# Recurrence and gated MLP on one core: from the ninth chunk on, score matmuls and output matmuls of two chunks stand next to each other

## The chip, the cores and the metric

One core of one Trainium2 chip. The metric is the device time of one execution in microseconds (us); the times given are of the whole program, the trace is of one profiled execution.

## The reference

A linear recurrence over 768 steps for 4 batches and 8 heads of 48, and behind it a gated MLP over the 3072 rows that come out.

```
for t in range(S):                       # S = 768, per batch and head, state is 48 x 48
    cur = einsum(u * k[t], v[t])
    y[t] = einsum(r[t], state + cur)
    state = w[t][:, None] * state + einsum(k[t], v[t])
x = y as (3072, 384)
out = (silu(x @ w_gate) * (x @ w_val)) @ w_out      # 384 -> 1536 -> 384
```

## The kernel before

**The recurrence** is cut into 24 chunks of 128 steps. Chunk n is chunk n // 4 of batch n % 4, so four chunks in a row belong to four batches and don't need each other; chunk n needs the state that chunk n - 4 left. For a chunk the names in the code are:

- `ws`, `kr`, `nat`, `vt`: the loads of decay, keys and receptances, the same in natural order, values.
- `scan`, `seed`, `kq`, `scan2`, `re`: running products of the decay and what is scaled by them, on DVE; `ru`, `ruk`, `a0`: the bonus on the diagonal, on DVE; `zero`: a small memset on POOL.
- `diag` (ACT): writes the diagonal into two tiles `at`, one for each half of the heads. `sc` (PE): the scores, 32 matmuls with 48 rows and 64 columns of the array, into two PSUM banks (j = 0 and 1). `pred` (DVE): copies the lower triangle of one score bank into `at`, in three instructions (L518 once, L524 twice); with that the bank is free.
- `kb` (PE, four transposes), `kn` (ACT, its copy), `dl` (PE, 32 small matmuls): the state's increment. `sps` (DVE) scales the state, `spb` (ACT) copies it into the zero-padded tile `sp`, `st` (DVE) adds the increment, with which the bank of `dl` is free.
- `vz` (ACT): a zero-padded copy of part of the values. `y` (PE): the output of the chunk, 56 matmuls of 32 columns. `xh` (ACT) and `xl` (DVE): the output split in a high and a low part, with which the bank of `y` is free.

**The MLP** runs over seven groups of 4, 2, 4, 4, 4, 4 and 2 chunks (`GROUPS`), each in twelve steps f. `gv` (PE): nine matmuls of 128 by 128 with 512 columns (256 for a group of 2), twice, for gate and value. `silu` and `hh` (ACT), `sg` and `hl` (DVE) make the product and split it. `po` (PE): three matmuls with 384 columns for each chunk of the group, added up over f in one PSUM bank for each chunk. `ob` and `out` bring out the group's result. `raw`, `top`, `low`, `shift`, `sign`, `plus`, `upper`, `lower` turn the weights' 64-bit bits into two parts while the first group runs; the bits lie in two buffers `raw` of 9216 bytes a partition.

**PSUM** has eight banks: two `pa` (for `kb`, `y`, `dl`), two `gv` (for the gate and value products and, from chunk 6 on, for `sc`), four `po`.

**The order** of all this is one table, `ORDER`, of 1495 words such as `gv:2:5:0` (group, step, gate or value) or `sc:13` (chunk). Every engine gets its instructions in the order of this table; nothing is moved later. `spin:6` stands for six matmuls whose result nobody reads.

Of the kernel before, what the change touches and what calls it, by code (L numbers as in the profile page):

```python
# [52 lines left out]
top:1 spin:7 wm:0:0 wl:0:0 kn:2 diag:2:1 zero:2 prod:3 scan:3 wm:0:2 wl:0:2 wm:0:1 wl:0:1 y:1 xh:1
sc:2 dl:2 xm:1 diag:2:0 raw:2 vt:3 ws:4 kr:4 kq:3 shift:1 seed:3 sign:1 plus:1 pred:2:0 pred:2:1
st:2 spin:2 kb:3 xl:1 low:2 whole:3 gv:0:0:0:a gv:0:0:1:a upper:1 scan2:3 kn:3 vz:2 wm:1:1 zero:3
y:2 silu:0:0:a diag:3:1 re:3 sc:3 sg:0:0:a scan:4 xh:2 diag:3:0 pred:3:1 pred:3:0 wm:1:2 wm:1:0
hh:0:0:a vz:3 top:2 hl:0:0:a prod:4 wl:1:2 whole:4 y:3 xh:3 seed:4 raw:3 po:0:0:c0 xm:2 xm:3
po:0:0:c1 wl:1:1 xl:2 xl:3 dl:3 wl:1:0 gv:0:0:0:b top:3 shift:2 sign:2 gv:0:0:1:b kq:4 plus:2
silu:0:0:b upper:2 scan2:4 sg:0:0:b hh:0:0:b low:3 gv:0:1:0:a kb:4 gv:0:1:1:a lower:2 hl:0:0:b
silu:0:1:a shift:3 sg:0:1:a po:0:0:c3 gv:0:1:0:b gv:0:1:1:b hh:0:1:a vt:4 vt:5 sign:3 ws2:0 kn:4  # L60
vz:4 check2:0 hl:0:1:a raw:4 plus:3 silu:0:1:b po:0:1:a prod:5 raw:5 upper:3 sg:0:1:b hh:0:1:b re:4
top:4 lower:3 po:0:0:c2 shift:4 gv:0:2:0 st:3 low:4 gv:0:2:1 hl:0:1:b silu:0:2 diag:4:0 sc:4 sign:4
sps:4 sg:0:2 diag:4:1 hh:0:2 plus:4 pred:4:0 pred:4:1 raw:6 gv:0:3:1 gv:0:3:0 upper:4 spb:4 lower:4
hl:0:2 dl:4 y:4 ws:5 top:5 silu:0:3 xh:4 low:5 shift:5 sign:5 sg:0:3 po:0:1:b plus:5 zero:4 hh:0:3
hl:0:3 scan:5 upper:5 po:0:2 lower:5 gv:0:4:0 top:6 silu:0:4 low:6 shift:6 xm:4 gv:0:4:1 gv:0:5:1
sign:6 sg:0:4 ws2:4 plus:6 whole:5 hh:0:4 xl:4 upper:6 raw:7 kq:5 raw:8 hl:0:4 top:7 lower:6 po:0:3
gv:0:5:0 shift:7 kb:5 silu:0:5 sg:0:5 sign:7 st:4 seed:5 low:7 vz:5 plus:7 gv:0:6:1 gv:0:6:0 scan2:5
zero:5 po:0:4 hh:0:5 kn:5 diag:5:1 top:8 upper:7 hl:0:5 lower:7 low:8 silu:0:6 shift:8 sg:0:6 sign:8
raw:9 po:0:5 hh:0:6 diag:5:0 gv:0:7:1 gv:0:7:0 plus:8 hl:0:6 re:5 upper:8 silu:0:7 lower:8 top:9
sg:0:7 sps:5 spb:5 po:0:6 gv:0:8:1 sc:5 gv:0:8:0 low:9 hh:0:7 raw:10 nat:6 shift:9 sign:9 plus:9  # L70
upper:9 kr:7 pred:5:1 pred:5:0 ws:6 vt:6 dl:5 y:5 raw:11 hl:0:7 kr:6 top:10 silu:0:8 lower:9
check2:4 sg:0:8 low:10 shift:10 sign:10 hh:0:8 plus:10 po:0:7 scan:6 upper:10 xh:5 top:11 hl:0:8
lower:10 gv:0:9:1 ws:7 gv:0:9:0 silu:0:9 po:0:8 shift:11 low:11 ub vt:7 sign:11 sg:0:9 gv:0:10:0
plus:11 hh:0:9 gv:0:10:1 xm:5 whole:6 upper:11 hl:0:9 kq:6 lower:11 po:0:9 xl:5 silu:0:10 ru:6
sg:0:10 ruk:6 gv:0:11:0 seed:6 scan2:6 hh:0:10 vz:7 zero:6 hl:0:10 silu:0:11 re:6 a0:6 kb:6
gv:0:11:1 kn:6 diag:6:0 sg:0:11 scan:7 hh:0:11 hl:0:11 po:0:10 dl:6 sc:6 sps:6 pred:6:0 diag:6:1
spb:6 nat:7 po:0:11:c2 po:0:11:c1 vz:6 gv:1:0:0 pred:6:1 ob:0:2 ru:7 st:6 seed:7 ws:8 silu:1:0
gv:1:0:1 kq:7 sg:1:0 hh:1:0 whole:7 ruk:7 hl:1:0 scan2:7 a0:7 po:0:11:c3 gv:1:1:0 gv:1:1:1
po:0:11:c0 out:0:2 y:6 zero:7 silu:1:1 ob:0:1 sg:1:1 diag:7:1 re:7 sc:7 po:1:0:c0 po:1:0:c1 nat:8
scan:8 hh:1:1 pred:7:1 sps:7 whole:8 diag:7:0 kr:8 hl:1:1 ru:8 pred:7:0 ruk:8 st:5 gv:1:2:0 po:1:1  # L80
seed:8 gv:1:2:1 spb:7 xh:6 silu:1:2 xl:6 sg:1:2 gv:1:3:0 a0:8 ws2:3 hh:1:2 hl:1:2 gv:1:3:1 silu:1:3
sg:1:3 hh:1:3 po:1:2 gv:1:4:0 gv:1:4:1 kq:8 hl:1:3 scan2:8 silu:1:4 gv:1:5:0 sg:1:4 hh:1:4 re:8
hl:1:4 kb:7 kn:7 ob:0:0 y:7 silu:1:5 diag:8:1 dl:7 st:7 diag:8:0 sc:8 pred:8:1 pred:8:0 po:1:3 sps:8
spb:8 gv:1:5:1 sg:1:5 zero:8 gv:1:6:0 po:1:4 hh:1:5 xh:7 ws:9 kb:8 scan:9 gv:1:6:1 nat:9 vt:9 vt:8
kr:9 seed:9 hl:1:5 whole:9 check2:3 ru:9 po:1:5 xl:7 vz:8 silu:1:6 gv:1:7:0 ruk:9 a0:9 sg:1:6
gv:1:7:1 hh:1:6 vz:9 kn:8 kq:9 hl:1:6 silu:1:7 scan2:9 y:8 dl:8 sg:1:7 ws:10 ws:11 diag:9:1 hh:1:7
nat:10 diag:9:0 zero:9 re:9 vt:10 hl:1:7 st:8 sc:9 sps:9 spb:9 pred:9:1 pred:9:0 kb:9 po:1:6 out:0:0
out:0:1 gv:1:8:0 gv:1:8:1 silu:1:8 kn:9 sg:1:8 hh:1:8 ru:10 hl:1:8 gv:1:9:1 gv:1:9:0 po:1:7 scan:10
ob:0:3 silu:1:9 xh:8 ruk:10 sg:1:9 seed:10 xl:8 y:9 dl:9 st:9 xh:9 xl:9 gv:1:10:0 gv:1:10:1 hh:1:9
hl:1:9 a0:10 kr:10 po:1:8 silu:1:10 po:1:9 whole:10 out:0:3 kq:10 sg:1:10 hh:1:10 scan2:10 gv:1:11:0  # L90
zero:10 hl:1:10 re:10 po:1:10 gv:1:11:1 silu:1:11 vt:11 nat:11 scan:11 ru:11 sg:1:11 hh:1:11 vz:10
diag:10:0 whole:11 gv:2:0:0 gv:2:0:1 hl:1:11 po:1:11:c0 po:1:11:c1 silu:2:0 diag:10:1 sg:2:0 ws2:6
ruk:11 seed:11 hh:2:0 gv:2:1:1 gv:2:1:0 hl:2:0 a0:11 kr:11 diag:11:0 silu:2:1 ob:1:1 sg:2:1 hh:2:1
check2:6 ob:1:0 po:2:0:c2 po:2:0:c0 nat:12 gv:2:2:0 ru:12 ruk:12 kq:11 hl:2:1 ws2:5 silu:2:2
gv:2:2:1 po:2:0:c3 sg:2:2 po:2:0:c1 sc:10 kb:10 sps:10 spb:10 kn:10 hh:2:2 scan2:11 pred:10:0 re:11
hl:2:2 po:2:1 pred:10:1 a0:12 check2:5 vz:11 gv:2:3:1 gv:2:3:0 ws2:2 ws:12 y:10 silu:2:3 xh:10
diag:11:1 sg:2:3 sps:11 spb:11 dl:10 st:10 hh:2:3 sc:11 kb:11 zero:11 pred:11:1 kn:11 pred:11:0
hl:2:3 po:2:2 gv:2:4:0 gv:2:4:1 silu:2:4 sg:2:4 xl:10 diag:12:0 gv:2:5:1 hh:2:4 dl:11 y:11 check2:2
# [6 lines left out]
pred:13:0 hl:2:7 xl:12 vt:15 vz:13 gv:2:8:0 gv:2:8:1 diag:14:1 silu:2:8 whole:14 sg:2:8 kq:14
scan2:14 dl:13 y:13 st:13 xh:13 xl:13 nat:15 zero:14 hh:2:8 re:14 gv:2:9:1 hl:2:8 diag:14:0 check:14
ws:15 ru:15 scan:15 gv:2:9:0 silu:2:9 po:2:7 sg:2:9 kr:15 kb:14 kn:14 sc:14 hh:2:9 vt:14 sps:14
pred:14:1 seed:15 spb:14 po:2:8 pred:14:0 hl:2:9 ruk:15 kq:15 whole:15 scan2:15 gv:2:10:0 out:1:1
re:15 a0:15 gv:2:10:1 silu:2:10 check:15 diag:15:1 vz:14 vz:15 po:2:9 sg:2:10 nat:16 hh:2:10 dl:14
st:14 y:14 hl:2:10 sps:15 zero:15 sc:15 pred:15:1 kb:15 diag:15:0 kn:15 pred:15:0 po:2:10 gv:2:11:0  # L110
spb:15 silu:2:11 gv:2:11:1 sg:2:11 ru:16 hh:2:11 xh:14 hl:2:11 ws:16 kr:16 gv:3:0:0 gv:3:0:1
po:2:11:c2 po:2:11:c1 scan:16 xl:14 silu:3:0 po:2:11:c3 sg:3:0 ob:2:1 hh:3:0 dl:15 y:15 po:2:11:c0
st:15 ob:2:2 xh:15 xl:15 gv:3:1:0 whole:16 ruk:16 hl:3:0 seed:16 gv:3:1:1 po:3:0:c0 silu:3:1 sg:3:1
kq:16 out:2:1 scan2:16 out:2:2 ws:17 vt:16 hh:3:1 po:3:0:c3 gv:3:2:1 gv:3:2:0 ob:2:0 ob:2:3 hl:3:1
silu:3:2 a0:16 nat:17 re:16 zero:16 ru:17 sg:3:2 diag:16:1 diag:16:0 po:3:0:c1 po:3:0:c2 hh:3:2
gv:3:3:0 hl:3:2 po:3:1 gv:3:3:1 silu:3:3 po:3:2 ruk:17 sg:3:3 check:16 hh:3:3 hl:3:3 out:2:3 sps:16
# [722 lines left out]
```

## Time and profile before

| | us |
|---|---|
| median of 3 runs | 569.04 (568.2 to 569.2) |
| the profiled execution's own time | 566.06 |
| its span in the trace | 564.4 |
| PE busy | 555.5 (98%) |
| PEld (weight loads, beside the matmuls) busy | 485.3 (86%) |
| DVE busy | 335.0 (59%) |
| ACT busy | 280.4 (50%) |

The span is the time from the first to the last instruction of one execution. A matmul's duration in the trace reaches to the modelled end of its pipeline, so neighbours overlap and a busy share of PE hides short pauses; the distance from one start to the next shows them.

### The profile page before, as it was taken

Reading aid. Unit: us, or ns where it says so; the run is one execution under the profiler, and the core shown is the slowest. Engines: PE = TensorE matmul, PEld = TensorE weight load, DVE = VectorE, ACT = ScalarE, POOL = GpSimd, SP = SyncE. Lnnn points to the kernel's source line nnn. Section 1 sums busy time; section 2 is a strip of 40 time slices with the busy share of each in tenths; the row PEclk is TensorE's granted clock in tenths of the full one; section 3 lists DMA queues with packets and bytes.
Section 4 is the critical chain, followed back from the end, with each engine's and each line's share of the span. In section 5 each row is a group of like instructions: output and inputs, shape, how many; then the busy total and the mean of one; then the engine's idle time right before and its main releaser. Section 6 shows DMA issues by size and latency. Waiting matters only on the chain.

```text
span 564.4 us, 12505 instructions
## 1 busy us (share of the span) xinstructions
PE 555.5 (98%) x5167; PEld 485.3 (86%) x5167; DVE 335.0 (59%) x602; ACT 280.4 (50%) x647; POOL 4.5 (1%) x35
## 2 busy tenths in 40 slices
...
GB/s 285 274 162 164 202 168 220 118 59 81 125 151 95 83 58 130 93 62 79 61 42 78 66 72 51 65 132 1 120 16 65 91 27 32 0 1 1 29 30 33
DMA packets 41598, 51.09 MB, mean 91 GB/s; under 512 B 12416, under 2 KB 30208, under 8 KB 41536
## 3 DMA queue, kind: packets, MB, share of 16 engines
...
q8 instruction: 42, 0.69, 0.5%
...
## 4 chain that ended last, share of the span: by engine, by line
PE 75%; DMA 1%; DVE 1%; SPq 0%; issue 0%; DVEq 0%
PE gv L625 43%; PE po L664 22%; PE y L576 5%; PE sc L500 2%; PE kb L472 1%; PE dl L544 1%; DMA nat<-in_nat_dram 1%; SPq L371 0%; DVE nat L438 0%; DVE ob L680 0%; DVE at L524 0%; DVE nat L441 0%; DVE at L518 0%; DVE x L603 0%; DVE st L553 0%
## 5 line engine op out<-in xcount | busy, mean ns | idle before, releaser
L625 PE MATMUL gv<-x,w_h 128*128 128x512 f32 (+1 forms) x984 | 282.6, 362 | 0.4 <-DVE sg L638 0.4
L625 PEld LDWEIGHTS gv<-x,w_h 128*128 128x128 f32 x984 | 176.5, 188 | 29.9 <-issue 1.5
L625 PE MATMUL gv<-x,w_l 128*128 128x512 f32 (+1 forms) x492 | 177.0, 360 | 0.0
L638 DVE TENSOR_TENSOR sg<-sg,gv 128x512 f32<-128x512 f32 (+1 forms) x82 | 49.9, 608 | 133.7 <-PE gv L625 83.9
L625 PEld LDWEIGHTS gv<-x,w_l 128*128 128x128 f32 x492 | 92.5, 188 | 12.3
L635 ACT ACTIVATE sg<-gv 128x512 f32<-128x512 f32 (+1 forms) x82 | 43.9, 535 | 118.1 <-PE gv L625 100.3
L664 PE MATMUL po<-w_h,hh 128*128 128x384 f32 x280 | 96.4, 344 | 0.0
L664 PE MATMUL po<-w_h,hl 128*128 128x384 f32 x280 | 94.4, 337 | 0.0
L664 PE MATMUL po<-w_l,hh 128*128 128x384 f32 x280 | 94.2, 336 | 0.0
L643 ACT ACTIVATE hh<-sg 128x512 fp32r<-128x512 f32 (+1 forms) x82 | 46.4, 566 | 94.4 <-DVE sg L638 82.5
L648 DVE TENSOR_TENSOR hl<-sg,hh 128x512 fp32r<-128x512 f32 (+1 forms) x82 | 49.8, 608 | 24.0 <-ACT hh L643 23.5
L664 PEld LDWEIGHTS po<-w_h,hh 128*128 128x128 f32 x280 | 52.5, 188 | 2.8 <-issue 0.4
L664 PEld LDWEIGHTS po<-w_h,hl 128*128 128x128 f32 x280 | 52.6, 188 | 1.8
L664 PEld LDWEIGHTS po<-w_l,hh 128*128 128x128 f32 x280 | 52.5, 188 | 0.0
L388 DVE TENSOR_TENSOR_SCAN qt<-ws,d 112x516 f32<-112x516 f32 x24 | 29.5, 1228 | 10.5 <-DMA ws<-in_wt_dram 10.2
L410 DVE TENSOR_TENSOR_SCAN et<-ws,d 112x516 f32<-112x516 f32 x24 | 29.5, 1229 | 1.9 <-ACT pend L393 1.3
L457 ACT ACTIVATE at<-ident,a 128x128 f32<-128x128 f32 x72 | 24.7, 392 | 10.6 <-PE y L576 8.8
L518 DVE COPY_PREDICATED at<-masks,sc 128x256 f32<-128x256 uint32 x36 | 16.1, 447 | 18.6 <-PE sc L500 16.7
L576 PE MATMUL y<-at,vz 128*32 128x128 f32 x384 | 25.3, 273 | 0.0
L454 ACT ACTIVATE at<-ident,a 128x128 f32<-128x128 f32 x72 | 24.6, 390 | 0.0
L524 DVE COPY_PREDICATED at<-masks,sc 64x128 f32<-64x128 uint32 x72 | 21.2, 295 | 0.5
L576 PEld LDWEIGHTS y<-at,vz 128*32 128x32 f32 x384 | 20.9, 110 | 0.0
...
## 6 DMA issues: line engine op xcount, KB each, us to landing
...
```

What stands on the lines that cost most here:

```text
L388: keep(nc.vector.tensor_tensor_scan(_flat(qts[n])[:, ::-1], wss[n][:, 1:][:, ::-1], _flat(d1)[:, ::-1], 0.0, ALU.mult, ALU.add))
L410: keep(nc.vector.tensor_tensor_scan(_flat(ets[n]), wss[n][:, :L], _flat(d1), 0.0, ALU.mult, ALU.add))
L454: keep(nc.scalar.activation(a[:, p, :], ident, AF.Copy, scale=d))
L457: keep(nc.scalar.activation(o, i[:, ::-1], AF.Copy, scale=d))
L524: keep(nc.vector.copy_predicated(a[o, p, :e], m.unsqueeze(1).to_broadcast([e, TWO, e]), s[o, p, :e],))
L576: pin(nc.tensor.matmul(ys[n][32 * q : 32 * q + 32, b // 4, :], lhs, rhs, start=start[q] == i, stop=stop[q] == i,))
L625: pin(nc.tensor.matmul(ps, a[:, f, j, q * P : (q + 1) * P], x[:, q, lo * P : hi * P], start=m == 0, stop=m == 3 * NK - 1,))
L635: keep(nc.scalar.activation(sgs[g, f, h], ps, AF.Silu))
L638: keep(nc.vector.tensor_tensor(sgs[g, f, h], sgs[g, f, h], gvs.pop((g, f, 1, h)), ALU.mult))
L643: keep(nc.scalar.activation(hhs[g, f, h], t, AF.Copy))
L648: keep(nc.vector.tensor_tensor(hls[g, f, h], t, hhs[g, f, h].bitcast(F32), ALU.subtract))
L664: pin(nc.tensor.matmul(pos[g, j], a[:, ts], x[:, f, 2, :], start=f == 0 and i == 0, stop=f == NF - 1 and i == 2,))
```

## The change

It concerns chunks from 8 on (`PAIRED`). Chunks 8 and 9, 10 and 11, up to 22 and 23 go through PE two at a time: the scores of both stand next to each other in `ORDER`, later the outputs of both and, where a state still has to be carried on, the increments of both. For that, the two chunks need buffers side by side: the odd chunk's scores go to the two `pa` banks, all increments from chunk 8 on go to the `gv` banks, and a second set of SBUF tiles (two `kr`, two `vt`, two `vz`, one `at`, one `kn`, one `sp`) is laid into the two `raw` buffers once the weights are converted. Three POOL memsets clear `vz` and `sp` there. No instruction of the chunks or of the MLP is added or removed; two more `spin` matmuls stand in the first stage (42 for 40). The table `ORDER` is another one from its 13th word on.

```diff
+PAIRED = 8
 ORDER = """
-ws:0 kr:0 scan:0 whole:0 spin:8 uh seed:0 prod:0 kq:0 spin:1 kb:0 scan2:0 kn:0 diag:0:0 kr:1 ws:1
...
-gv:2:7:1 scan2:13 spb:12 zero:13 hl:2:6 silu:2:7 dl:12 y:12 diag:13:1 re:13 st:12 sg:2:7 hh:2:7
-sc:13 ruk:14 kb:13 sps:13 spb:13 a0:14 kn:13 check:13 po:2:6 pred:13:1 scan:14 kr:14 seed:14 xh:12
...
+sps:12 sg:2:6 scan2:14 a0:14 sc:13 sc:12 pred:13:0 pred:13:1 po:2:5 check:14 kb:13 diag:12:0 spb:12
+pred:12:1 kr:15 vt:14 kn:13 hh:2:6 pred:12:0 y:13 y:12 dl:13 dl:12 nat:15 ws:15 vt:15 xh:13 hl:2:6
...
+    lates = {}
+    def late(name):
+        if not lates:
+            for i, parts in enumerate((
+                (("kr0", 2 * NPR * C), ("kr1", 2 * NPR * C), ("vz0", NPR * 48)),
+                (("at", NPR * C), ("kn", NPR * PR), ("sp", 2 * NPR * D), ("vt0", H * D), ("vt1", H * D), ("vz1", NPR * 48)),
+            )):
+                t = wst.tile([P, 3, DM, 2], I32, tag="raw", name=f"late_{i}")
+                t, lo = t.rearrange("p i c t -> p (i c t)").bitcast(F32), 0
+                for k, w in parts:
+                    lates[k], lo = t[:, lo : lo + w], lo + w
+            for k in ("vz0", "vz1", "sp"):
+                keep(nc.gpsimd.memset(lates[k], 0.0))
+        return lates[name]
+    def apart(n):
+        return n >= PAIRED and n % 4 > 1
...
     def kr(n):
+        if apart(n):
+            krs[n] = late(f"kr{n % 2}")[:PR].rearrange("d (i p c) -> d i p c", i=2, p=NPR)
...
-            own = (psA, "pa", 2) if n < SCORED else (psM, "gv", 2)
+            own = (psA, "pa", 2) if n < SCORED or n >= PAIRED and n % 2 else (psM, "gv", 2)
...
-        dls[n] = psA.tile([P, NPR, D], F32, tag="pa", name=f"dl_{n}")
+        own = (psA, "pa", 2) if n < PAIRED else (psM, "gv", 2)
+        dls[n] = own[0].tile([P, NPR, D], F32, tag=own[1], name=f"dl_{n}", bufs=own[2])
```

**PE at chunks 12 and 13.** Before, the last output matmuls of chunk 12 stand ahead of the first score matmuls of chunk 13; chunk 12's own scores were a stretch of their own that ended 54 rows earlier.

```order
L576 MATMUL y_12_3017<-at_12_0_2724,vt_12_2835 32x128
L576 MATMUL y_12_3017<-at_12_0_2724,vz0_95 32x128
L576 MATMUL y_12_3017<-at_12_1_2912,vt_12_2835 32x128
L576 MATMUL y_12_3017<-at_12_1_2912,vz0_95 32x128 x4
L500 MATMUL sc_13_0_3056<-kr_13_2929 64x128
L500 MATMUL sc_13_1_3057<-kr_13_2929 64x128
L500 MATMUL sc_13_0_3056<-kr_13_2929 64x64
```

With the change the scores of chunk 13 are followed by those of chunk 12, and these by the MLP's `po`:

```order
L534 MATMUL sc_13_0_2950<-kr_13_2646 64x128
L534 MATMUL sc_13_1_2951<-kr_13_2646 64x128
L534 MATMUL sc_12_0_2968<-kr_12_2541 64x128
L534 MATMUL sc_12_1_2969<-kr_12_2541 64x128
L534 MATMUL sc_12_0_2968<-kr_12_2541 64x64
...
L534 MATMUL sc_12_1_2969<-kr_12_2541 64x128
L704 MATMUL po_2_0_2529<-w_h_109,hh_2_5_2909 128x384
```

In one stretch there are now 64 score matmuls; the outputs of both chunks and then their increments follow in another, behind `po:2:5` and the transposes `kb:13`:

```order
L616 MATMUL y_13_3033<-late_1_1900,vt_13_2679 32x128
L616 MATMUL y_13_3033<-late_1_1900,vz1_97 32x128 x4
L616 MATMUL y_12_3062<-kr_12_2541,sp_93 32x128 x12
...
L616 MATMUL y_12_3062<-at_12_1_2939,vz0_95 32x128 x4
L584 MATMUL dl_13_3091<-vt_13_2679,late_1_1900 32x48 x3
...
L584 MATMUL dl_12_3108<-vt_12_2642,kn_12_2907 16x48
L503 MATMUL kb_14_3143<-ident_81,late_0_1899 128x112 x4
L665 MATMUL gv_2_7_0_3148<-x0_2_1659,w_h_109 128x512
```

**DVE at chunks 8 and 9.** Before, chunk 9's score banks are read by two `pred` (rows L518 and L524), between the state's update and the product of the MLP's step 8:

```order
L553 TENSOR_TENSOR st_0_111<-dl_8_2063,st_0_111 112x192
L530 TENSOR_TENSOR st_1_112<-st_1_112,pend_108 112x192
L518 COPY_PREDICATED at_9_1_2085<-masks_86,sc_9_1_2111 128x4x64
L524 COPY_PREDICATED at_9_1_2085<-masks_86,sc_9_1_2111 64x2x64 x2
L518 COPY_PREDICATED at_9_0_2096<-masks_86,sc_9_0_2110 128x4x64
L524 COPY_PREDICATED at_9_0_2096<-masks_86,sc_9_0_2110 64x2x64 x2
L638 TENSOR_TENSOR sg_1_8_2170<-sg_1_8_2170,gv_1_8_1_2160 128x256
```

With the change four `pred` stand in a row; chunk 8's banks, which the MLP's next products need, are read by the first and the third of them:

```order
L688 TENSOR_TENSOR hl_1_8_2096<-sg_1_8_2072,hh_1_8_2083 128x256
L552 COPY_PREDICATED at_8_1_1909<-masks_86,sc_8_1_2099 128x4x64
L558 COPY_PREDICATED at_8_1_1909<-masks_86,sc_8_1_2099 64x2x64 x2
L552 COPY_PREDICATED at_9_0_2040<-masks_86,sc_9_0_2116 128x4x64
L558 COPY_PREDICATED at_9_0_2040<-masks_86,sc_9_0_2116 64x2x64 x2
L552 COPY_PREDICATED at_8_0_1923<-masks_86,sc_8_0_2098 128x4x64
L558 COPY_PREDICATED at_8_0_1923<-masks_86,sc_8_0_2098 64x2x64 x2
L552 COPY_PREDICATED late_1_1900<-masks_86,sc_9_1_2117 128x4x64
L558 COPY_PREDICATED late_1_1900<-masks_86,sc_9_1_2117 64x2x64 x2
L466 TENSOR_TENSOR nat_10_2055<-nat_10_2055,u_bc_106 128x384
L678 TENSOR_TENSOR sg_1_9_2165<-sg_1_9_2165,gv_1_9_1_2167 128x256
```

Two `pred` more stand between a score stretch and the DVE's next step for the MLP.

## Rows read from the trace of the kernel before

**Rows 1.** The page: busy us (share of the span) and instructions.

```profile
PE 555.5 (98%) x5167; PEld 485.3 (86%) x5167; DVE 335.0 (59%) x602; ACT 280.4 (50%) x647; POOL 4.5 (1%) x35
```

**Rows 2.** Waits of PE: us in total, times, longest.

```profile
PE gv L625 <- DVE sg L638: 0.4, 1, 0.4
PE kb L472 <- issue: 0.3, 1, 0.3
PE kb L472 <- ACT st L551: 0.2, 1, 0.2
```

**Rows 3.** Timeline of PE (start, duration), increments and output of a chunk between products.

```profile
302.44 0.40 PE L625 MATMUL gv<-x,w_l 128*128 128x512 f32 x1
302.68 0.39 PE L625 MATMUL gv<-x,w_h 128*128 128x512 f32 x1
303.00 0.54 PE L544 MATMUL dl<-vt,kn 128*32 128x48 f32 x32
303.36 0.83 PE L576 MATMUL y<-kr,sp 112*32 112x128 f32 x24
...
305.00 0.50 PE L625 MATMUL gv<-x,w_h 128*128 128x512 f32 x1
305.33 0.39 PE L625 MATMUL gv<-x,w_l 128*128 128x512 f32 x1
```

**Rows 4.** Timeline of PE, scores of a chunk by themselves.

```profile
331.80 0.34 PE L664 MATMUL po<-w_h,hl 128*128 128x384 f32 x1
331.98 0.34 PE L664 MATMUL po<-w_l,hh 128*128 128x384 f32 x1
332.25 0.90 PE L500 MATMUL sc<-kr 48*64 48x128 f32 x32
333.08 0.60 PE L472 MATMUL kb<-ident,kr 112*128 112x112 f32 x4
333.45 0.42 PE L664 MATMUL po<-w_h,hh 128*128 128x384 f32 x1
```

**Rows 5.** Timeline of PE, output, increments and scores in one stretch.

```profile
396.89 0.86 PE L576 MATMUL y<-kr,sp 112*32 112x128 f32 x24
397.57 0.28 PE L576 MATMUL y<-at,vt 128*32 128x128 f32 x1
...
398.44 0.52 PE L544 MATMUL dl<-vt,kn 128*32 128x48 f32 x32
398.90 0.90 PE L500 MATMUL sc<-kr 48*64 48x128 f32 x32
399.73 0.44 PE L664 MATMUL po<-w_h,hh 128*128 128x384 f32 x1
400.01 0.33 PE L664 MATMUL po<-w_h,hl 128*128 128x384 f32 x1
```

**Rows 6.** Timeline of PE, first output matmuls of a chunk and the scores behind them.

```profile
256.74 0.83 PE L576 MATMUL y<-kr,sp 112*32 112x128 f32 x24
...
258.38 0.90 PE L500 MATMUL sc<-kr 48*64 48x128 f32 x32
```

**Rows 7.** Timeline of PE, increments ahead of the MLP's products.

```profile
165.08 0.52 PE L544 MATMUL dl<-vt,kn 128*32 128x48 f32 x32
165.53 0.39 PE L625 MATMUL gv<-x,w_h 128*128 128x256 f32 x1
```

**Rows 8.** Timeline of DVE, the two `pred` of chunk 9.

```profile
156.75 0.45 DVE L518 COPY_PREDICATED at<-masks,sc 128x256 f32<-128x256 uint32 x1 [0.21 <-PE sc L500]
...
157.73 0.45 DVE L518 COPY_PREDICATED at<-masks,sc 128x256 f32<-128x256 uint32 x1
158.08 0.60 DVE L524 COPY_PREDICATED at<-masks,sc 64x128 f32<-64x128 uint32 x2
```

**Rows 9.** Timeline of PE, the products `gv:1:8:0` behind those scores.

```profile
158.13 0.28 PE L625 MATMUL gv<-x,w_h 128*128 128x256 f32 x1
```

**Rows 10.** Timeline of PE, spins in the first stage.

```profile
12.30 1.46 PE L701 MATMUL idle<-masks 128*128 128x512 bf16 x6
```

More of the change, by code (lines that the diff above doesn't have):

```diff
@@ L53 @@
[L53 to L98, printed above, removed]
@@ L105 @@
[L105 to L116, printed above, removed]
@@ L158 @@
[L158 to L162 removed]
+ws:0 kr:0 scan:0 whole:0 spin:8 uh seed:0 prod:0 kq:0 spin:1 kb:0 scan2:0 zero:0 kn:0 diag:0:0 kr:1
@@ new lines @@
+diag:2:0 raw:2 vt:3 ws:4 kr:4 kq:3 shift:1 seed:3 sign:1 plus:1 pred:2:0 pred:2:1 st:2 spin:3 kb:3
+xl:1 low:2 whole:3 gv:0:0:0:a gv:0:0:1:a upper:1 scan2:3 zero:3 kn:3 vz:2 wm:1:1 y:2 silu:0:0:a
+diag:3:1 re:3 sc:3 sg:0:0:a scan:4 xh:2 diag:3:0 pred:3:1 pred:3:0 wm:1:2 wm:1:0 hh:0:0:a vz:3 top:2
+hl:0:0:a prod:4 wl:1:2 whole:4 y:3 xh:3 seed:4 raw:3 po:0:0:c0 xm:2 xm:3 po:0:0:c1 wl:1:1 xl:2 xl:3
+dl:3 wl:1:0 gv:0:0:0:b top:3 shift:2 sign:2 gv:0:0:1:b kq:4 plus:2 silu:0:0:b upper:2 scan2:4 zero:4
@@ new lines @@
+sg:0:0:b hh:0:0:b low:3 gv:0:1:0:a kb:4 gv:0:1:1:a lower:2 hl:0:0:b silu:0:1:a shift:3 sg:0:1:a
+po:0:0:c3 gv:0:1:0:b gv:0:1:1:b hh:0:1:a vt:4 vt:5 sign:3 ws2:0 kn:4 vz:4 check2:0 hl:0:1:a raw:4
+plus:3 sps:4 silu:0:1:b po:0:0:c2 ws:5 po:0:1:a sg:0:1:b top:4 gv:0:2:1 upper:3 re:4 hh:0:1:b
+gv:0:2:0 scan:5 lower:3 hl:0:1:b shift:4 sign:4 st:3 diag:4:1 silu:0:2 low:4 sg:0:2 sc:4 hh:0:2
+plus:4 spb:4 raw:5 hl:0:2 pred:4:1 upper:4 top:5 whole:5 po:0:1:b gv:0:3:1 lower:4 shift:5 sps:5
+gv:0:3:0 raw:6 low:5 silu:0:3 dl:4 po:0:2 diag:4:0 sign:5 sg:0:3 hh:0:3 low:6 vz:5 seed:5 plus:5
@@ new lines @@
+sg:0:7 sign:9 po:0:6 hh:0:7 plus:9 kr:7 vt:7 hl:0:7 kq:6 top:10 gv:0:8:0 gv:0:8:1 upper:9 ru:6
+silu:0:8 lower:9 sg:0:8 shift:10 po:0:7 kb:6 raw:11 low:10 hh:0:8 xh:5 kn:6 ws2:3 gv:0:9:0 gv:0:9:1
+hl:0:8 sign:10 plus:10 ruk:6 silu:0:9 upper:10 dl:6 po:0:8 top:11 sg:0:9 vz:6 lower:10 shift:11
+low:11 gv:0:10:1 gv:0:10:0 sign:11 hh:0:9 plus:11 hl:0:9 seed:6 check2:3 upper:11 a0:6 lower:11
+whole:6 po:0:9 xm:5 silu:0:10 sg:0:10 scan2:6 hh:0:10 zero:6 ws:7 hl:0:10 re:6 scan:7 diag:6:0
+gv:0:11:0 ws:8 gv:0:11:1 silu:0:11 xl:5 sg:0:11 hh:0:11 sps:6 seed:7 spb:6 nat:7 hl:0:11 gv:1:0:1
@@ new lines @@
+y:15 xh:15 xl:15 kq:16 scan2:16 nat:17 kr:17 ws:17 hh:3:0 zero:16 vt:17 y:14 dl:15 dl:14 st:15 ru:17
+ruk:17 st:14 re:16 kb:16 po:2:11:c1 po:2:11:c3 ob:2:1 gv:3:1:0 check:16 ob:2:2 diag:16:0 vt:18
+out:2:1 out:2:2 hl:3:0 scan:17 silu:3:1 xh:14 kq:17 seed:17 gv:3:2:0 gv:3:1:1 po:2:11:c0 sg:3:1
+hh:3:1 po:3:0:c0 whole:17 hl:3:1 kn:16 a0:17 xl:14 scan2:17 silu:3:2 po:3:0:c3 gv:3:2:1 kb:17 ob:2:3
+sg:3:2 ob:2:0 po:3:0:c2 po:3:0:c1 diag:17:0 hh:3:2 sps:16 hl:3:2 gv:3:3:0 silu:3:3 kr:18 kr:19
+zero:17 ws:18 spb:16 kn:17 po:3:1 re:17 vz:17 sc:16 sc:17 nat:18 diag:16:1 po:3:2 pred:16:0
```

167 lines of the change are left out of this document (107 added, 60 removed).

## The prediction

> **What bounds the kernel now.** The page comes first: PE is busy for 98% of the span, DVE for 59%, ACT for 50% [rows 1]. Since matmuls overlap in the trace, that share alone does not show that PE never pauses. The view of waits does: behind the start-up PE waited for another engine three times, for 0.4, 0.3 and 0.2 us [rows 2]. So from the first product on the time is the sum of the distances between PE's starts, and an engine beside it matters only where it makes PE wait. The timeline of PE then shows what these distances are made of. Products follow each other every 0.24 us, output matmuls of the MLP every 0.18 us. Where PE goes over to the recurrence's small matmuls and back, the distances grow, though nobody is waited for:
>
> - Going in: 0.32 us from a product to the first `dl` [rows 3], 0.27 us from a `po` to the first `sc` [rows 4]; that is 0.09 us above the usual distance.
> - Coming back: the first full matmul is followed after 0.33 us [rows 3] or 0.28 us [rows 5], 0.10 us above the usual. So a small stretch costs 0.19 us at its two ends, whatever is in it.
> - Inside, the price hangs on what comes next. `dl` takes 0.36 us ahead of `y`, which uses 32 columns as well [rows 3], but 0.45 us ahead of full matmuls [rows 7] and 0.46 us ahead of scores [rows 5]. `y` takes 1.55 us ahead of `dl` [rows 5], 1.64 us ahead of full matmuls [rows 3] and of scores [rows 6]. `sc` takes 0.83 us ahead of full matmuls, in a stretch of its own [rows 4] and behind `dl` [rows 5]. Where the form changes, a piece thus lasts some 0.1 us longer: the array finishes what it has begun.
>
> **The change, part by part.** The work stays; the places where PE changes its form are counted in the two tables.
>
> *Stretches.* Before there are 35 (12 with what belongs to chunks 0 to 7, 23 behind), with the change 31 (14 and 17). The first stage gets two more, since `dl:4` and `y:4` as well as `dl:6` and `sc:6` no longer touch; behind it there are eight for scores, eight for outputs, and `y:7 dl:7`. 4 x 0.19 = 0.76 us less.
>
> *Outputs.* 17 `y` stood ahead of another form, now 8 do; of the nine others eight stand ahead of another `y` and one more ahead of `dl`. The `dl` case saves 0.09 us. `y` ahead of `y` is not in the trace. Its lower bound is that same 0.09; the upper bound is the 0.19 us by which a score stretch's modelled end, less one matmul of 0.28 us as the `y` in rows 5 has it, lies before the next start (0.90 - 0.28 = 0.62 us against 0.83, less 0.02 for the next start) [rows 4, 5]. I take the middle, 0.14: 8 x 0.14 + 0.09 = 1.2 us less (0.8 to 1.6).
>
> *Scores.* 24 `sc` stood ahead of another form, now 16 do. With the same bounds, 8 x 0.14 = 1.1 us less (0.7 to 1.5).
>
> *Increments.* 11 `dl` stood ahead of another form, now 13 do: 2 x 0.09 = 0.2 us more. Seven times fewer does `dl` stand ahead of `y`; a row behind another `dl` instead is worth no more than 0.02 us each and is left out.
>
> The sum is -0.76 - 1.2 - 1.1 + 0.2 = -2.9 us (-2.1 to -3.7).
>
> *Spins.* Two more; six take at most 1.46 us [rows 10], so up to 0.5 us for both. Both stand in the first stage ahead of places that DVE and ACT set: there PE waits at two `kb` for 0.3 and 0.2 us [rows 2], and that wait takes them in. I take 0; without that cover it is 0.5.
>
> *Where a bank comes free.* This is the price of the change. A pair of score stretches fills the two `gv` banks and the two `pa` banks, and the next product needs a `gv` bank. One `pred` takes 0.98 us [rows 8], four in a row 3.9 us. In the trace the first product behind the scores starts at 158.13 us, while the second `pred` still runs until 158.68 [rows 8, 9]: it needs only the bank that was read first. From the end of the first score piece of a pair, with DVE free and 0.2 us until it wakes [rows 8], the first `pred` is through after 1.2 us, the second after 2.2, the third after 3.1. PE meanwhile has 0.83 us of the other scores and one `po` of the table: twelve matmuls of 0.18 in a group of four chunks, six in a group of two. The first product thus wants its bank after 0.8 + 2.2 = 3.0 us (1.9 in the group of two), the second 2.1 us (1.1) later. At six of the eight pairs the first product has at least 0.8 us to spare, as the table has a bank of the even chunk read first or second; the second product has less, where other DVE steps stand between the `pred`. Two pairs are tight by these numbers. At chunks 8 and 9, a group of two, the even chunk's banks are read first and third: the second product wants its bank after 3.0 us and gets it after 3.1. At 20 and 21 the odd chunk's banks are read first and the even chunk's third, after 3.1 us against 3.0. I take 0.1 us for each and 0.2 us for whatever else is late: +0.4 us. The lower end is 0; at the upper end, should PE wait for all four (4.1 us), it is 1.1 us a pair and 2.2 us at chunks 8 and 9, 10 us.
>
> Here a rule stands against the change: the Trainium skill, TensorEngine Tiling (Array Packing), section Performance Considerations, says that tiling makes TensorE faster but not the emptying of PSUM, which can become the bottleneck. The trace agrees as to the ratio: DVE needs 1.96 us for the scores that PE makes in 0.83 [rows 4, 8]. By that rule at its worst the sum would be -2.9 + 10 = +7 us; by the row with the early product [rows 9] it is -2.9 + 0.4. I go by the row, and the rule is the third rival.
>
> *Increments in `gv` banks.* `dl` needs a bank that `silu` or `sg` gives back; two `y`, 3.1 us [rows 5], lie between the last product and the first `dl` at five of the six pairs that have increments, and a `po` at the sixth. The next product waits for `st`, one DVE step behind `dl`; a `po` of 2.1 us covers it, and at chunks 12 and 13 the other `dl` and `kb`, 0.46 + 0.37 us [rows 4, 5]. Nothing is charged. If the cover failed, it would be one step of 0.4 us or so at the pairs with `dl`.
>
> *Loads and memsets.* The second set of buffers lets loads start earlier, and the three memsets lie on POOL, which is busy for 1% [rows 1]. If a load comes late after all, it shows as a wait of DVE, not charged here.
>
> Sum: -2.9 + 0 + 0.4 = -2.5 us. The profiled execution took 566.06 us with a span of 564.4; the span becomes 561.9, its own time 563.6. The median of the three runs is 569.04, 3 us above the profiled execution; the same 2.5 us off it give 566.5.
>
> **The rivals.**
>
> 1. *More falls away.* The one wait of a product, 0.4 us [rows 2], sat in a part of the table that is new; if it goes, no bank is late, and the same-form price is at the upper bound, it is -3.7 - 0.4 = -4.1 us: 564.9. For it speaks that PE hardly waited before; against it that two pairs are tight on paper.
> 2. *The gain is given back.* If every pair waits 0.36 us for a bank, 8 x 0.36 = 2.9 us are gone: 569.0. For it speaks that DVE also has the MLP's steps to do between the `pred`; against it the 0.8 us to spare for the first product at six pairs. Its milder form, half of that and the lower bound of the drains, gives about 567.9.
> 3. *Slower.* Emptying PSUM becomes the bound: DVE comes to the `pred` a step late, so that PE waits for the whole row of four, 1.1 us a pair and 2.2 at chunks 8 and 9: -2.9 + 10 = +7, 576. It decides from 0.36 us of wait a pair on. Against it speaks that DVE is idle for 41% of the span [rows 1] and woke up for these `pred` from a wait for PE [rows 8], so it was ahead of PE there.
> 4. *The change does less than it says*: same-form neighbours save as little as 0.09 us. Then the drains give 2.1 us and the time is 567.3; that lies in the forecast's own range.
>
> **How the numbers follow.** Forecast 566.5 with 0.58 (its own range 565.4 to 567.6); more falls away 0.09; the milder form of the second rival 0.10; gain given back 0.13; slower 0.10. A measurement of this kernel can tell about 0.2%, 1.1 us, from no change, so faster means below 567.9: 0.58 + 0.09 + 0.10 = 0.77; same 0.13; slower 0.10. The range leaves out the slower case and the lowest twentieth: 564.7 to 569.5.
>
> **What the profile of the changed kernel would show.** The span is about 562 us. In PE's timeline there are eight groups of 64 `sc` that take some 1.5 us (0.83 + 0.69) where two took 1.66, and two `y` behind each other that take about 3.1 us. A same-form neighbour that lasts 0.83 or 1.64 all the same would prove the term wrong. The view of waits should have PE waits for `pred` and `sg` of below 1 us in all; several of 0.3 us or more, or DVE with more work just ahead of the `pred`, would be the second or third rival. A wait of PE in the first stage, where the table is new too, would be a cause that I have not priced.

## The result and the profile after

The changed kernel takes 563.78 us (median of five executions, 562.14 to 564.76), the kernel before in the same session 568.20 us (five, 566.78 to 569.20): the ratio is 0.9919 (95% interval 0.9901 to 0.9936), 4.4 us less. The forecast was 2.5 us less and 566.5 us; the time lies 0.9 us below the low end of the range. In a second session the same two kernels gave 564.27 us (six executions) and 568.04 us (22), 3.8 us less.

The profiled execution of the changed kernel took 564.76 us, the longest of its five, while that of the kernel before, 566.06 us, lies below all five of its own; these two profiles are thus only 1.3 us apart, and the account below goes by stretches inside them. The page shows the busy line that answers to [rows 1]:

```profile
PE 554.1 (98%) x5169; PEld 486.5 (86%) x5169; DVE 335.4 (60%) x602; ACT 279.1 (50%) x647; POOL 5.8 (1%) x38
```

Nothing in this line tells where 4 us went; PE is as full as before. The view of PE's waits answers to [rows 2] (us in total, times, longest); the first is the start-up:

```profile
PE idle L741 <- POOL masks L245: 2.6, 1, 2.6
PE dl L584 <- issue: 0.2, 1, 0.2
PE gv L665 <- DVE sg L678: 0.2, 1, 0.2
```

The product wait of 0.4 us of [rows 2] is gone, another of 0.2 us has come, and no wait for a `pred` stands in this view. It measures from the modelled end of the matmul before, so short waits are read from one start to the next here. The turns show in PE's timeline (start, duration), first the scores of chunks 8 and 9 with the products behind them:

```profile
158.35 0.33 PE L704 MATMUL po<-w_l,hh 128*128 128x384 f32 x1
158.62 1.57 PE L534 MATMUL sc<-kr 48*64 48x128 f32 x64
160.12 0.44 PE L704 MATMUL po<-w_h,hh 128*128 128x384 f32 x1
...
161.28 0.28 PE L665 MATMUL gv<-x,w_h 128*128 128x256 f32 x1
...
162.22 0.69 PE L665 MATMUL gv<-x,w_h 128*128 128x256 f32 x2
162.74 0.28 PE L665 MATMUL gv<-x,w_l 128*128 128x256 f32 x1
```

64 score matmuls take 1.50 us (158.62 to 160.12), where two chunks apart took 0.83 us each [rows 4]: the neighbour saves 0.16 us. The pair of `gv` at 162.22 lasts 0.69 us where others last 0.40: inside it the second product (`gv:1:9:1`) begins, and it waits for its bank. DVE's timeline shows for what:

```profile
159.58 0.44 DVE L552 COPY_PREDICATED at<-masks,sc 128x256 f32<-128x256 uint32 x1 [0.45 <-PE sc L534]
...
161.52 0.45 DVE L552 COPY_PREDICATED at<-masks,sc 128x256 f32<-128x256 uint32 x1
161.86 0.60 DVE L558 COPY_PREDICATED at<-masks,sc 64x128 f32<-64x128 uint32 x2
```

The third `pred`, which gives chunk 8's second bank back, ends at 162.46; the product starts right behind it, 0.19 us later than its rhythm (from one start to the next, as recorded in ns). At chunks 20 and 21, the other pair that the prediction called tight, it is 0.27 us. The outputs and increments of chunks 9 and 8, on PE again:

```profile
165.69 0.28 PE L665 MATMUL gv<-x,w_h 128*128 128x256 f32 x1
165.90 0.86 PE L616 MATMUL y<-kr,late 112*32 112x128 f32 x24
...
167.46 0.84 PE L616 MATMUL y<-kr,sp 112*32 112x128 f32 x24
...
168.99 0.52 PE L584 MATMUL dl<-vt,late 128*32 128x48 f32 x32
169.33 0.52 PE L584 MATMUL dl<-vt,kn 128*32 128x48 f32 x32
169.78 0.60 PE L503 MATMUL kb<-ident,late 112*128 112x112 f32 x4
```

Two `y` take 3.09 us up to the first `dl`, as forecast (3.1).

### The profile page after: what moved, and what is told of

It reads as the page before. It is cut to its first block, busy times and chain, and to the rows that moved or that the text cites. A ratio compares the mean times of both kernels' runs of the same rounds, so it can differ in the third digit from the quotient of the medians.

```text
span 562.9 us, 12512 instructions
## 1 busy us (share of the span) xinstructions
PE 554.1 (98%) x5169; PEld 486.5 (86%) x5169; DVE 335.4 (60%) x602; ACT 279.1 (50%) x647; POOL 5.8 (1%) x38
## 4 chain that ended last, share of the span: by engine, by line
PE 96%; DMA 1%; DVE 1%; SPq 1%; POOL 0%; issue 0%; DVEq 0%; POOLq 0%
PE gv L665 51%; PE po L704 27%; PE y L616 6%; PE sc L534 2%; PE idle L741 2%; PE kb L503 2%; PE dl L584 1%; PE sc L541 1%; DMA late<-in_kr_dram 1%; PE wm L326 1%; PE kb L505 1%; PE gv_0b L665 0%; PE gv_1a L665 0%; PE gv_0a L665 0%; PE gv_1b L665 0%
## 5 line engine op out<-in xcount | busy, mean ns | idle before, releaser
L488 ACT ACTIVATE at<-ident,a 128x128 f32<-128x128 f32 x56 | 19.2, 391 | 1.2 <-DVE a L473 1.2
L632 ACT ACTIVATE x<-y 128x384 fp32r<-128x384 f32 x24 | 11.5, 484 | 16.1 <-PE y L616 16.0
L552 DVE COPY_PREDICATED at<-masks,sc 128x256 f32<-128x256 uint32 x28 | 12.5, 447 | 11.5 <-PE sc L534 11.0
L452 ACT ACTIVATE ws<-ws 112x517 f32<-112x517 f32 x24 | 15.2, 632 | 8.1 <-DVE et L438 8.0
L485 ACT ACTIVATE at<-ident,a 128x128 f32<-128x128 f32 x56 | 19.1, 389 | 0.0
L643 DVE TENSOR_TENSOR x<-y,x 128x384 fp32r<-128x384 f32 x18 | 9.9, 554 | 14.8 <-ACT x L632 14.8
```

Source lines behind the costliest of these rows:

```text
L452: keep(nc.scalar.activation(w, w, AF.Square))
L485: keep(nc.scalar.activation(a[:, p, :], ident, AF.Copy, scale=d))
L488: keep(nc.scalar.activation(o, i[:, ::-1], AF.Copy, scale=d))
```

## The experiments

In all of them "body" is the stretch of a profile from the first product's start to the last matmul's start. The stage ahead of it lasted between 28.9 and 31.2 us in these profiles, and 30.2 us in the second profiles of both kernels (`b_again` and `a_again`). What the two more spins cost, up to 0.5 us by the prediction, can't be told within this scatter, and body lengths compare better than spans. They are 529.7 us before (530.3 in the second profile) and 526.7 changed (526.0 in the second; the first has 0.5 us of a wait inside the increments at 229.5 us, which the second has not). So the bodies differ by 3.0 to 4.4 us, as the profiles are paired. The runs below fall into three sessions, in which the kernel before took 568.04, 567.82 and 568.22 us; each ratio is to the kernel before in the same session.

**Both kernels once more (`b_again`, `a_again`).** No edit.

> The kernel before, once more, to see where its executions differ. Theory 1 (counted turns): from the first product to the end of the span it takes 535.5 us again, within 0.3; what differs between executions lies ahead of the first product, where the clock is granted at its lower level in some of them for a few us (the changed kernel's profiled execution shows that at 6.7 to 10.6 us: four spins take 1.87 us there, against 1.02 before). Theory 2 (the profiled execution of before was a lucky one): PE waits behind the first product that the first profile did not have, for 1 to 1.5 us in all, or a span of 537 us behind the first product.

> The changed kernel, once more. Theory 1: 532.7 us from the first product to the end, within 0.3, so 2.9 us less than before, and the ratio of the times is 0.994 to 0.995 when both have as many executions with the lower clock. Theory 2: the ratio stays near 0.992, and the part behind the first product is below 532 us.

Measured: 568.06 us (567.34 to 569.45, ratio 1.0004, 0.9994 to 1.0013) and 564.27 us (563.84 to 565.66, ratio 0.9946, 0.9933 to 0.9958). The effect is 3.8 to 4.4 us; the 569.04 us of the three runs ahead of the prediction was a high draw, 0.8 us over the median of five. The ratio is the one of theory 1, but both stretches from the first product to the end miss its bounds: 536.4 us in `b_again` (535.5 expected, within 0.3) and 531.8 us in `a_again` (532.7, within 0.3). In `b_again` 0.6 us of that lies in short waits, among them the product wait, which from start to start is 0.71 us beyond the usual distance there and 0.55 us in the first profile. So single waits differ between executions of one kernel too. Four spins take 1.02 us in both second profiles, as before, and 1.87 us in the first one of the changed kernel; the view by stretches gives a granted clock of 1.00 there, so the lower level is read from the longer durations alone.

**Scores apart again (`s_split`).** Three `po` matmuls stand between the two chunks' scores, at all eight pairs; the rest of the change stays. At chunks 8 and 9:

```diff
-... sc:8 sc:9 pred:8:1 pred:9:0 pred:8:0 pred:9:1 po:1:8 ...
+... sc:8 po:1:8:c0 sc:9 pred:8:1 pred:9:0 pred:8:0 pred:9:1 po:1:8:c1 ...
```

> The changed kernel with three matmuls of the neighbouring po (one chunk's part) moved in between the two score pieces of each of the eight pairs; nothing added. Theory 1: eight stretches more, each 0.19 us at its ends and 0.14 to 0.16 us for the score piece that stands ahead of another form again: 2.6 to 2.8 us more than the changed kernel. If the gain comes from earlier loads and buffers, the split costs below 1 us.

Measured: 566.98 us (565.80 to 568.68), ratio 0.9986 (0.9974 to 0.9998), 2.7 us over `a_again`. Its PE timeline at the same place:

```profile
158.24 0.33 PE L707 MATMUL po<-w_l,hh 128*128 128x384 f32 x1
158.50 0.90 PE L537 MATMUL sc<-kr 48*64 48x128 f32 x32
159.33 0.44 PE L707 MATMUL po<-w_h,hh 128*128 128x384 f32 x1
159.61 0.34 PE L707 MATMUL po<-w_h,hl 128*128 128x384 f32 x1
159.78 0.34 PE L707 MATMUL po<-w_l,hh 128*128 128x384 f32 x1
160.05 0.90 PE L537 MATMUL sc<-kr 48*64 48x128 f32 x32
160.88 0.45 PE L707 MATMUL po<-w_h,hh 128*128 128x384 f32 x1
```

Each chunk takes 0.83 us again; with 0.27 us into the second stretch instead of 0.18, and 0.28 us instead of 0.18 behind the first, a split costs 0.16 + 0.09 + 0.10 = 0.35 us, eight of them 2.8 us. The prediction's prices were 0.19 for a stretch and 0.14 for the lost neighbour, 0.33. The body is 3.0 us longer than that of `a_again`.

**Outputs apart again (`o_split`, mended in `o_split2`).** The same between the two `y` of each pair:

```diff
-... y:9 silu:1:10 ob:0:3 y:8 xh:9 dl:9 ...
+... y:9 po:1:9:c0 silu:1:10 ob:0:3 y:8 xh:9 dl:9 ...
```

> The changed kernel with three matmuls of a po moved in between the two output pieces of each pair. Theory 1: eight stretches more, 0.19 us at the ends and 0.15 us for the y: 2.7 us more than the changed kernel (2.2 if y ahead of y is worth only the 0.09 us that y ahead of dl is). If buffers are what counts, below 1 us.

> The changed kernel with three po matmuls between the two y of each of the eight pairs again; at chunks 20 and 21 they now come from po:4:6, whose product is ready, instead of po:4:7. Theory 1 (the price is the turn of the array: 0.19 us for a stretch and 0.14 us for y that loses its neighbour): 8 x 0.33 = 2.6 us more than the changed kernel, no PE wait of 1 us or more, the two y of a pair 1.67 us each to the next full matmul. Rival A (the neighbours are worth little, and what o_split lost was all due to the moved po): within 0.5 us of the changed kernel. Rival B (splitting outputs costs more than turns, since xh and xl of the first y then collide with something): over 4 us more.

`o_split` took 572.64 us (571.52 to 573.35), ratio 1.0088 (1.0074 to 1.0103), 8.4 us over `a_again`; its body is 6.7 us longer, where 2.7 was expected. The view of waits has one new long wait, since the `po` that I had moved at chunks 20 and 21 needs an `hh` that is not there yet.

```profile
PE po L707 <- ACT hh L686: 2.6, 1, 2.6
```

Behind it the table by stretches (us, then PE, PEld, DVE, ACT and POOL busy, the granted clock, the DMA share) shows the granted clock at 0.56 and 0.59:

```profile
410.00:418.00 8.00, 5.07 (x74) 3.61 (x76) 2.71 (x4) 3.36 (x8) 0.11 (x1) 1.00 0.51 146
418.00:420.00 2.00, 2.00 (x48) 2.00 (x52) 0.56 (x1) 0.82 (x2) 0.00 (x0) 0.56 0.71 194
420.00:422.00 2.00, 2.00 (x20) 1.43 (x13) 0.56 (x1) 0.49 (x1) 0.00 (x0) 0.59 0.75 233
422.00:424.00 2.00, 2.00 (x11) 1.74 (x10) 0.45 (x1) 0.00 (x0) 0.00 (x0) 1.00 0.01 3
```

The wait and 1.7 us lost at the lower clock (3.4 us at half speed) make up what the turns don't explain.

`o_split2` takes the `po` from a step that is ready: 566.26 us (565.41 to 567.02), ratio 0.9969 (0.9959 to 0.9979). In the body it is 2.2 us over `a_again`, 0.4 us below the 2.6 expected; about as much goes by shorter distances between full matmuls (last part of this section). At chunks 9 and 8 the first `y` now lasts 1.67 us to the next full matmul and the second 1.56 us to `dl`:

```profile
165.35 0.86 PE L619 MATMUL y<-kr,late 112*32 112x128 f32 x24
167.02 0.44 PE L707 MATMUL po<-w_h,hh 128*128 128x384 f32 x1
...
167.74 0.86 PE L619 MATMUL y<-kr,sp 112*32 112x128 f32 x24
169.30 0.52 PE L587 MATMUL dl<-vt,late 128*32 128x48 f32 x32
```

1.67 + 1.56 - 3.09 = 0.14 us: the price that was taken for `y` ahead of `y`. Theory 1 holds for the scores and for the outputs; rival A, that neighbours are worth little, falls, and so does rival B, over 4 us.

**The banks read in the wrong order (`bank_late`).** Four pairs read the odd chunk's banks first:

```diff
-pred:8:1 pred:9:0 pred:8:0 pred:9:1
+pred:9:0 pred:9:1 pred:8:1 pred:8:0
```

> The changed kernel with the even chunk's score banks, which the next products need, read after the odd chunk's at four pairs (8/9, 10/11, 14/15, 18/19); the same instructions. Theory 1 (the product waits until the pred that frees its bank is through; all else as before): by the DVE's rows of the changed kernel the first product behind the scores comes 1.1 us later at 8/9, 2.1 at 10/11 over both products, 0.25 at 14/15 and 2.8 at 18/19: 6.2 us more than the changed kernel, slower than the kernel before; more by up to 2 us if the granted clock falls behind the longest wait. Rival (PSUM's emptying is no bound in any order, since PE has other work): no difference over 1 us.

Measured: 575.56 us (573.77 to 576.89), ratio 1.0142 (1.0123 to 1.0162). The view of waits, and PE's timeline at chunks 18 and 19:

```profile
PE gv L665 <- DVE at L558: 6.9, 4, 2.3
```

```profile
384.07 0.34 PE L704 MATMUL po<-w_l,hh 128*128 128x384 f32 x1
386.36 0.47 PE L665 MATMUL gv<-x,w_h 128*128 128x512 f32 x1 [1.95 <-DVE at L558]
386.67 0.45 PE L665 MATMUL gv<-x,w_l 128*128 128x512 f32 x1
386.92 1.06 PE L665 MATMUL gv<-x,w_h 128*128 128x512 f32 x2
387.77 0.63 PE L665 MATMUL gv<-x,w_l 128*128 128x512 f32 x1
...
390.32 0.40 PE L665 MATMUL gv<-x,w_l 128*128 128x512 f32 x1
```

Four waits of 0.8 to 2.3 us have come: 6.9 us in the view, 7.8 us from start to start with the 0.3 us of one second product. At these four pairs the order of the change has one, of 0.19 us. Single pairs are 0.7 to 0.9 us off what was expected, to both sides (at 8 and 9 it is more, since the first `pred` now needs the scores that come second). Behind the product at 386.36 the distances double from 0.23 to 0.43 us for 3.4 us: the granted clock is at 0.5 there, the lower level of 1.2 GHz, and once more behind the wait of 1.8 us at chunks 8 and 9, so that it costs 1.7 us twice. 7.8 + 2 x 1.7 = 11.2 us; the body grew by 11.3. This is the third rival of the prediction, brought about by the order of the `pred` alone. The Trainium skill, TensorEngine Tiling (Array Packing), Performance Considerations, says that tiling speeds up TensorE and not the emptying of PSUM, which may become the bottleneck. The trace agrees for this order of the instructions, with 7.8 us of waits; in the order of the change they are 0.45 us.

**The product wait of before taken away (`b_nowait`).** In the kernel before, DVE's `sg:1:2` moves ahead of three other steps:

```diff
-xh:6 silu:1:2 xl:6 sg:1:2 gv:1:3:0
+xh:6 silu:1:2 sg:1:2 st:5 seed:8 xl:6 gv:1:3:0
```

> The kernel before with sg of the second group's step 2 ahead of three other DVE steps (st:5, seed:8, xl:6), so that the one product wait of 0.4 to 0.5 us behind the first stage goes. Theory 1: that wait is worth its whole length: 0.55 to 0.7 us off the body of the span (first product to last matmul), 0.1% of the time, and no other distance changes; the changed kernel's gain thus holds this much that has nothing to do with pairs. Rival: the wait comes back at the next product or at xl, st: 0 us.

Measured: 566.94 us (566.42 to 568.36), ratio 0.9991 (0.9979 to 1.0003): not told apart from no change. PE's timeline says why:

```profile
134.53 0.70 PE L625 MATMUL gv<-x,w_h 128*128 128x256 f32 x2
...
137.07 0.34 PE L664 MATMUL po<-w_h,hh 128*128 128x384 f32 x1
137.47 0.44 PE L664 MATMUL po<-w_h,hl 128*128 128x384 f32 x1
```

Of the 0.55 us of start-to-start delay 0.19 us came back one product earlier and 0.23 us at a `po` that waits for the next DVE step. The wait was worth 0.1 us there, the body is 529.8 us as before, and the rival is nearer than theory 1.

**A version with three waits less (`a_best`).** In the changed kernel both banks of chunk 8 are read first, chunk 20's scores and `pred` come ahead of chunk 21's, and `sg:1:11` stands ahead of the next chunk's loads:

```diff
-sc:8 sc:9 pred:8:1 pred:9:0 pred:8:0 pred:9:1
+sc:8 sc:9 pred:8:1 pred:8:0 pred:9:0 pred:9:1
-silu:1:11 gv:2:0:0 po:1:10 ws2:5 zero:10 ru:11 ruk:11 scan:11 kq:11 sg:1:11
+silu:1:11 sg:1:11 gv:2:0:0 po:1:10 ws2:5 zero:10 ru:11 ruk:11 scan:11 kq:11
-sc:21 pred:21:0 pred:21:1 ws2:2 sc:20 pred:20:0 po:4:5 hl:4:6 kq:22 pred:20:1
+sc:20 pred:20:0 pred:20:1 ws2:2 sc:21 pred:21:0 po:4:5 hl:4:6 kq:22 pred:21:1
```

> The changed kernel with its three largest PE waits behind the first stage (0.19, 0.26 and 0.26 us beyond the usual distance) taken away by the order of DVE's steps: at 8/9 both banks of the even chunk are read first, at 20/21 the even chunk's scores and pred come first, and sg of the second group's last step stands ahead of the next chunk's loads. Theory 1 (the waits are worth their length): 0.7 us less than the changed kernel. Rival (the banks' order is hidden, or the moved pred makes something else late): no less, or more.

Measured: 563.52 us (563.17 to 563.65), ratio 0.9927 (0.9914 to 0.9941), where `a_again` has 0.9946 (0.9933 to 0.9958). The body is 525.24 us, 0.71 us shorter than that of `a_again`, as theory 1 has it; at 162.22 the pair of `gv` that lasted 0.69 us is back at its usual duration:

```profile
162.23 0.40 PE L665 MATMUL gv<-x,w_h 128*128 128x256 f32 x2
162.46 0.28 PE L665 MATMUL gv<-x,w_l 128*128 128x256 f32 x1
```

**Scores with no transposes behind them (`b_kbapart`, `b_kbfirst`).** Turns and waits left about 1.1 us of the gain over. It sits where nothing was to change: between full matmuls inside their runs. The mean distances from one start to the next behind 125 us, in ns, runs with a wait left out, are

```
                      po, 384 columns   gv, 512 columns
kernel before              175.76            230.63
  second profile           175.77            230.62
  b_nowait                 175.78            230.62
changed kernel             174.79            229.84
  a_again                  174.79            229.88
  s_split                  174.70            229.78
  o_split2                 174.65            229.35
  a_best                   174.67            229.80
b_kbapart                  175.06            229.71
b_kbfirst                  175.10            229.71
```

With some 590 and 770 distances, 0.97 and 0.76 ns are 0.57 + 0.58 = 1.1 us. A run of full matmuls of one kind comes in one of a few rhythms, and mostly keeps it until PE turns to another kind. In the kernel before it was the slowest, 176.5 and 233.3 ns, in seven of the nine stretches that begin with `sc` and then `kb`: 172 distances between products of 512 columns. (Of the other two, one has products of 256 columns, and the one behind chunk 18 goes from 233 to 229 ns and back, each time behind a run of `po`.) Another 60 of 233.2 ns stand behind scores with no `kb`, at 480 us. The changed kernel has `kb` right behind scores once (`sc:6 kb:7`). So in the kernel before nine `kb` were moved, behind the next `po` (five of them with their copies `kn`) or, in the second kernel, ahead of the scores:

```diff
-sc:16 ... kb:16 po:3:3
+sc:16 ... po:3:3 kb:16
```

> The kernel before, with the nine kb that stand right behind a chunk's scores (chunks 9 to 18 but 14) moved behind the next po, so that a po and not a transpose follows the scores. Seen so far: PE's full matmuls run in rhythms that last from one turn to the next; in the kernel before, po comes every 176.5 ns and gv every 233.3 ns in all stretches that begin with sc and kb, against 173.4 to 174.7 and 228.9 to 229.4 ns in most others, and the changed kernel has hardly any sc with kb behind it. Theory 2 (the slow rhythm comes from scores with kb right behind them, and this is the about 1.1 us of the gain that no turn and no wait explains): po's mean distance falls from 175.7 ns to below 175.0 and that of gv with 512 columns from 230.3 to below 229.8, 1.1 us less in all; against it stand nine turns that cost 0.14 us more each, +1.3: by the clock about the time of before. Rival (the rhythm goes by chance, with the exact moment at which PE starts again): mean distances that stay, or change without regard to kb; +1.3 us or any other sum.

> The kernel before, with the same nine kb moved ahead of the scores: the scores are followed by po here too, and kb still lies in the same stretch. Theory 2 (it is kb right behind the scores): as in b_kbapart, po below 175.0 ns and gv below 229.8 ns on the mean; turns +0.14 us at nine places and +0.09 where dl or y now stand ahead of kb and not of sc (four places): +1.6 us, less 1.1: 0.5 us more than before. Variant (kb anywhere in the stretch brings the slow rhythm): means as in before, +1.6 us. Rival (chance): means that change without regard to kb.

`b_kbapart` took 567.33 us against 568.22 (ratio 0.9975, 0.9958 to 0.9991), `b_kbfirst` 569.69 (1.0028, 1.0012 to 1.0045). The last rows of the table show the means near where theory 2 wanted them: that of the products is below its bound, that of `po` 0.06 and 0.10 ns above. One stretch, the products behind chunk 17's scores, first of the kernel before:

```profile
333.08 0.60 PE L472 MATMUL kb<-ident,kr 112*128 112x112 f32 x4
...
336.12 0.63 PE L625 MATMUL gv<-x,w_h 128*128 128x512 f32 x2
...
340.32 0.63 PE L625 MATMUL gv<-x,w_h 128*128 128x512 f32 x2
```

and of `b_kbapart`:

```profile
337.01 0.55 PE L472 MATMUL kb<-ident,kr 112*128 112x112 f32 x4
...
337.86 0.62 PE L625 MATMUL gv<-x,w_h 128*128 128x512 f32 x2
...
341.98 0.62 PE L625 MATMUL gv<-x,w_h 128*128 128x512 f32 x2
```

Both pairs of rows have 18 distances between them: 4.20 us and 4.12 us. In both kernels all 172 of these distances are gone, and the 60 at 480 us, where nothing was moved, keep 233.2 ns. The runs of `b_kbapart` are 1.14 us shorter in all: 0.95 us in stretches right behind scores or `kb`, 0.27 us behind outputs that the edit left alone, and 0.08 us longer behind increments.

So `kb` right behind scores brought most of the 233 ns rhythm of the kernel before. It does not follow that the changed kernel's 1.1 us has this cause alone. That kernel has distances of 233 ns too, 95 in its first profile and 121 in the second, behind `dl` or `kb`, and what stands ahead of a run doesn't settle its rhythm: the same products in the same order have 21 distances of 229.5 ns in the first profile (first two rows) and of 233.3 ns in `a_again` (last two):

```profile
275.24 0.63 PE L665 MATMUL gv<-x,w_h 128*128 128x512 f32 x2
280.06 0.62 PE L665 MATMUL gv<-x,w_h 128*128 128x512 f32 x2
```

```profile
274.43 0.63 PE L665 MATMUL gv<-x,w_h 128*128 128x512 f32 x2
279.33 0.63 PE L665 MATMUL gv<-x,w_h 128*128 128x512 f32 x2
```

And `o_split2`, where no scores and no `kb` moved, has products 0.5 ns closer together than `a_again`, 0.4 us in all. So the rival of chance, the moment at which PE starts again, has a part in it that no run here parts from the rest.

In `b_kbapart` the nine further turns cost 0.5 us and not 1.3 (`kb` behind `sc` had a first distance of its own that is 0.055 us longer, which the expectation had left out). `b_kbfirst` has the same shorter distances, and loses more than they give to a new wait: `kb` stands three times ahead of a bank that `st` has yet to free:

```profile
PE kb L472 <- DVE st L553: 1.4, 3, 0.5
```

It came out 1.5 us over the kernel before, where 0.5 was expected.

## Why the prediction was right in direction and wrong in size

Set up from every start-to-start distance, the bodies of the kernel before and of `a_again`, the two profiles with the fewest chance waits, differ by 3.76 us:

| part | forecast | measured |
|---|---|---|
| turns (entering, leaving, one form behind another) | -2.9 | -2.8 |
| score banks late | +0.4 | +0.45 |
| other PE waits behind the first stage | 0 | -0.3 |
| distances between full matmuls in their runs | not in the sum | -1.1 |

- **Turns.** Right, in sum and in both prices that were not in the trace: 0.16 us for `sc` (0.14 taken), 0.14 for `y`, shown by the two splits. The forecast's stretches, drains and neighbours are the mechanism of three quarters of the gain. That "the array finishes what it has begun" where the form changes is a reading; the runs show the price, not the reason.
- **Spins.** 0 was taken. It is 30.2 us up to the first product in both second profiles, but 28.9 and 30.2 us in the first ones; whether it is 0 or the 0.5 us of the forecast's other case, these profiles don't tell.
- **Banks.** The two pairs called tight are the two that wait, 0.19 and 0.27 us where 0.1 each and 0.2 for the rest were charged. `bank_late` shows what the order was worth, `a_best` that these waits count in full.
- **The product wait.** The main forecast kept the wait of 0.4 us [rows 2]; the first rival let it go. It went (0.55 us from start to start), and a new one of 0.26 us at `gv:2:0:1` came, because DVE reaches `sg:1:11` late: -0.3 us net.
- **The step that failed** is the reading that "the time is the sum of the distances between PE's starts", of which only those at turns were taken to change: "products follow each other every 0.24 us, output matmuls of the MLP every 0.18 us" was used for both kernels, so that their change stood at nothing without a reason. They differ by 0.3 to 0.6%, 1.1 us in all. Rows with two digits don't show that; the mean over hundreds of starts does. `b_kbapart` and `b_kbfirst` show that `kb` right behind `sc` brought most of the 233 ns rhythm of the kernel before. How much of the changed kernel's 1.1 us that is, why PE should keep a slower rhythm, and what chooses among the rhythms elsewhere (in `a_again` the stretch behind 203 us runs at 176.6 and 233.3 ns with `dl` and `kb` ahead of it) stay open.
- **The level.** The forecast was put on the median of three runs, 569.04 us; five gave 568.20. That is 0.8 of the 2.7 us by which the time missed 566.5; 1.3 us are the parts above, and the rest lies within what single executions differ by. Put on 568.20, the same range would be 563.9 to 568.7, and 563.78 lies just under its lower edge: the miss of the range is in part ill luck with three executions, the 1.1 us are not.

Of the rivals the first came closest (564.9 us, 4.1 us less), for half its reasons: the product wait went, but banks were late and the prices were not at their upper bound. The second, third and fourth did not happen.
